# A linear-attention block and a gated feed-forward block in one kernel: how the start is fed, where M's last chunk is multiplied, and how the last token tile is split

## The chip, the cores and the metric

The kernel runs on one core of one Trainium2 chip. The core has a matrix engine (TensorE, PE in the profile; its weight loads are PEld), a vector engine (DVE), an activation engine (ScalarE, ACT), a general engine (GpSimd, POOL) and a queue engine (SyncE, SP), all with instruction streams of their own that wait for each other by semaphores. 16 DMA engines move data between HBM and the on-chip SBUF; matmuls write to PSUM, which has 8 banks. The metric is the device time of one execution in microseconds, lower is better.

## What is computed

`x` is 2048 tokens of 576 features in bf16. The output is `x` plus two branches that both start from the layer norm of `x`: a linear attention with 32 heads of 18 features, and a feed-forward block with 4608 hidden features.

```python
xn = layernorm(x)                                  # mean and variance over 576 features
q, k, v = split(xn @ wqkv)                         # 32 heads of 18
phi = lambda t: where(t > 0, t + 1, exp(t)) + 1e-6
kv  = einsum("bhsd,bhse->bhde", phi(k), v)         # 18 x 18 for each head
z   = sum over tokens of phi(k)
o   = einsum(phi(q), kv) / (einsum(phi(q), z) + 1e-6)
out = x + o @ wo + (gelu(xn @ w_gate) * (xn @ w_up)) @ w_down
```

## The kernel before

The kernel works in three stages on tiles of 128 tokens.

**Attention stage.** For each of 16 token tiles: load `x`, mean and variance (`bn_stats`, `bn_aggr`, VectorE), `rstd`, normalize into `xn`, transpose into `xnT` (on TensorE for the first two tiles, by DMA for the others), multiply by the k and q weights (four groups of five matmuls of 288 columns), apply phi (an exp on ScalarE, a min/max on VectorE), and accumulate `G = xn^T phi(k)`. kv follows from G at the end. `z` is added up on GpSimd. The instructions are put in order by a small list scheduler in the kernel that works with estimated durations; only the order of its steps reaches the engines. The loads and the layer norm:

```python
    load_x(0, 1)
    load_x(1, 1)
    nc.scalar.preload_act_table_set("natural_log_exp_and_others")
    load_w(1)
    load_x(2, 2)
    load_w(0)
    load_x(4, 4)
# ... (cut)
    def ln_rstd(n):
        r = rstd[:, n:n + 1]
        nc.gpsimd.tensor_scalar_add(out=r, in0=mv[:, n, 1:2], scalar1=EPS_LN)
        nc.gpsimd.tensor_tensor(out=r, in0=r, in1=mhalf[:], op=ALU.pow)

    def ln_bias(n):
        nc.gpsimd.tensor_scalar(
            out=nbias[:, n:n + 1], in0=mv[:, n, 0:1], scalar1=rstd[:, n:n + 1], scalar2=-1.0, op0=ALU.mult, op1=ALU.mult,
        )

    def ln_norm_act(n, c0=0, c1=D):
        nc.scalar.activation(
            out=xn[:, n, c0:c1], in_=x_sb[:, n, c0:c1], func=ACT.Identity, bias=nbias[:, n:n + 1], scale=rstd[:, n:n + 1],
        )

    def ln_norm(n, c0=0, c1=D):
        nc.vector.tensor_scalar(
            out=xn[:, n, c0:c1], in0=x_sb[:, n, c0:c1], scalar1=mv[:, n, 0:1], scalar2=rstd[:, n:n + 1],
            op0=ALU.subtract, op1=ALU.mult,
        )
```

The steps given to the scheduler, where `NORM` says for each token tile whether VectorE (D) or ScalarE (A) normalizes it:

```python
    def step(name, *args, **kw):
        steps[name] = _Step(*args, **kw)

    NORM = "DADADAAADAADAADA"
    COPY = ("DVE", "ACT")
# ... (cut)
    for n0 in range(8, NS, 2):
        step(("x", n0), "SP", 0.50, n0 - 5.5, [], lambda n0=n0: load_x(n0, 2), ready=1.6 * n0 + 2.0, tail=3.0)
    for n in range(NS):
        lead = {0: -9.0, 1: 0.5, 2: -0.5, 3: -0.5}.get(n, 0.0)
        after_x = [("x", n // 2 * 2)] if n >= 8 else []
        x_at = X_AT[n] if n < 8 else 0.0
        for h in range(2):
            step(("stats", n, h), "DVE", 0.41, n - 2.2 + lead, after_x, lambda n=n, h=h: ln_half(n, h), ready=x_at)
        step(("aggr", n), "DVE", 0.21, n - 2.1 + lead, [("stats", n, 0), ("stats", n, 1)], lambda n=n: ln_aggr(n))
        step(("rstd", n), "POOL", POW, n - 2.1 + lead, [("aggr", n)], lambda n=n: ln_rstd(n))
        if n < TD:
            for i, (k0, k1, eng) in enumerate([(0, 3, "ACT"), (3, KT, COPY[n])]):
                b = TP_BANK[n] - i
                if NORM[n] == "A":
                    if not i:
                        step(("bias", n), "POOL", 0.15, n - 2.1 + lead, [("rstd", n)], lambda n=n: ln_bias(n))
                    step(("norm", n, i), "ACT", (0.49, 0.36)[i], n - 2.1 + lead, [("bias", n)],
                         lambda n=n, k0=k0, k1=k1: ln_norm_act(n, k0 * P, min(k1 * P, D)))
                else:
                    step(("norm", n, i), "DVE", (0.27, 0.20)[i], n - 2.1 + lead, [("rstd", n)],
                         lambda n=n, k0=k0, k1=k1: ln_norm(n, k0 * P, min(k1 * P, D)))
# ... (cut)
                     lambda n=n, k0=k0, k1=k1, b=b, eng=eng: tp_copy(n, k0, k1, b, acopy if eng == "ACT" else vcopy))
            ready = [("xnT", n, 0), ("xnT", n, 1)]
        else:
            if NORM[n] == "A":
                step(("bias", n), "POOL", 0.15, n - 2.1, [("rstd", n)], lambda n=n: ln_bias(n))
                step(("norm", n), "ACT", 0.65, n - 2.1, [("bias", n)], lambda n=n: ln_norm_act(n))
            else:
                step(("norm", n), "DVE", 0.43, n - 2.1, [("rstd", n)], lambda n=n: ln_norm(n))
# ... (cut)
        if n > 0:
            idle = [("norm" if NORM[n + 4] == "D" else "bias", n + 4)] if n + 4 < NS else []
            step(("z", n), "POOL", 1.40, n + 2.0, [("phi", m, 1, h) for m in (0, n) for h in range(2)] + idle,
                 lambda n=n: z_add(n))
        step(("G", n), "PE", 0.75, n + 1.15, [("phi", n, 1, 0), ("phi", n, 1, 1)], lambda n=n: g_accumulate(n, G_A))
    step(("spin",), "PE", 0.11, -1.0, [("tp", 0, 1)], lambda: spin(2))

    step(("bmask",), "POOL", 0.95, 0.2, [("rstd", 2)], make_bmask)
    step(("g",), "POOL", 0.75, 0.3, [("rstd", 2)], clear_g)
```

**Gate/up stage.** It runs four times, for 512 tokens each: 18 blocks of two units, a unit being 18 matmuls of 64 rows by 512 columns. The array is split into two row tiles (partitions 0 to 63 and 64 to 127) that work at the same time on two PSUM banks. In `p1` one row tile adds to one bank and the other to the second; in `p2` they take the other bank each, after a no-op on another engine's queue has seen the last of `p1`:

```python
        def p1(self):
            for kt in self.first:
                self.mm(0, LO, kt, kt == self.first[0], False)
                last = self.mm(1, HI, kt, kt == self.first[0], False)
            self.turn = self.relay.nop()
            tc.add_manual_dep(self.turn.ins, last.ins.name, SYNC, reason="the row tiles take turns on a bank")

        def p2(self):
            for kt in self.then:
                m = self.mm(1, LO, kt, False, kt == self.then[-1])
                if kt == self.then[0]:
                    tc.add_manual_dep(m.ins, self.turn.ins.name, SYNC, reason="the bank's other row tile has written")
                self.mm(0, HI, kt, False, kt == self.then[-1])
# ... (cut)
            load_wo()
        elif sc == 0 and k >= 2:
            load_wd_slice()
        for i, (b, u) in enumerate(units):
            u.p2()
            gl = fwork.tile([P, SC], F32, name="gl")
            nc.scalar.activation(out=gl[:], in_=ps_all[:, b[0], :], func=ACT.Gelu_apprx_tanh)
            nc.vector.tensor_tensor(out=hT[:, GUB * k + i, :], in0=ps_all[:, b[1], :], in1=gl[:], op=ALU.mult)
```

During the first of the four, `M = kv @ wo` is made for the last four heads (72 rows) and copied to `m_last`, from which DMAs fill places in `m_sb`:

```python
    def load_wo():
        nc.sync.dma_start(wo2[:CR, 0:4, :], A_wo[0:4 * CR, :].rearrange("(c p) j -> p c j", p=CR))
        nc.sync.dma_start(wo2[:D - 4 * CR, 4, :], A_wo[4 * CR:D, :])
# ... (cut)
    def m_product(c, bank):
        rows = DH * HCH[c]
        for hf in range(2):
            b = bank(hf)
            hs = slice(hf * HALF, (hf + 1) * HALF)
            nc.tensor.matmul(
                ps_all[:rows, b, :HALF], lhsT=kvT[:rows, c, :rows], rhs=wo2[:rows, c, hs], start=True, stop=True,
            )
            nc.scalar.copy(out=m_sb[:rows, c, hs] if c < 4 else m_last[:rows, hs], in_=ps_all[:rows, b, :HALF])

    def m_last_product():
        two = [banks.next(), banks.next()]
        m_product(4, lambda hf: two[hf])

    def m_last_tails():
        for i in range(2):
            nc.sync.dma_start(m_sb[CR + i:CR + i + 1, 0:4, :], m_last[HP + 4 * i:HP + 4 * i + 4, :])

    def m_last_rows():
        for rows in (LO, HI):
            nc.sync.dma_start(m_sb[rows, 4, :], m_last[0:HP, :])

    m_last_steps = {4: m_last_product, 7: m_last_tails, 9: m_last_rows}
```

**Down stage.** For each of four token tiles, 36 matmuls with `w_down` and 4 with `M` for each half of 288 output columns, a pair of row-tiled matmuls for M's last chunk, the addition of `x`, and the store. The very last tile stores its halves apart:

```python

        def __init__(self, n):
            self.n, self.ts = n, slice(n * P, (n + 1) * P)
            self.banks = [banks.next(), banks.next()]
            self.opened = False
# ... (cut)
        def pair(self):
            for hf, rows in ((0, LO), (1, HI)):
                nc.tensor.matmul(
                    self.acc(hf), lhsT=pqT[rows, 4, self.ts], rhs=m_sb[rows, 4, HALVES[hf]],
                    start=not self.opened, stop=self.opened, skip_group_check=True,
                )
            self.opened = True
# ... (cut)
            for f in range(NF):
                if f in todo:
                    todo[f]()
                nc.tensor.matmul(
                    self.acc(hf), lhsT=hT[:, f, j * P:(j + 1) * P], rhs=wd_sb[:, f, HALVES[hf]],
                    start=(f == 0 and not paired), stop=False, skip_group_check=True,
                )
            for c in range(4):
                nc.tensor.matmul(
                    self.acc(hf), lhsT=pqT[:, c, self.ts], rhs=m_sb[:, c, HALVES[hf]],
                    start=False, stop=(paired and c == 3), skip_group_check=True,
                )

        def add(self, hf):
            if hf == 0:
                self.res = fwork.tile([P, D], BF16, name="res")
            hs = HALVES[hf]
            nc.vector.tensor_tensor(out=self.res[:, hs], in0=self.acc(hf), in1=x_sb[:, self.n, hs], op=ALU.add)
            if self.n == NS - 1:
                nc.sync.dma_start(out_view[:, self.n, hs], self.res[:, hs])
            elif hf == 1:
                nc.sync.dma_start(out_view[:, self.n, :], self.res[:])
```

Of the kernel before, what the change touches and what calls it, by code (L numbers as in the profile page):

```python
# [8 lines left out]
ACT = mybir.ActivationFunctionType  # L9
# [48 lines left out]
def kernel(  # L58
# [52 lines left out]
    load_x(1, 1)  # L111
# [9 lines left out]
    make_identity(nc, ident[:])  # L121
    eps_att = const.tile([P, 1], F32, name="eps_att")
    nc.vector.memset(eps_att[:], EPS_ATT)
    mhalf = const.tile([P, 1], F32, name="mhalf")
    nc.vector.memset(mhalf[:], -0.5)
# [12 lines left out]
    kvT = persist.tile([P, NCH, CR], BF16, name="kvT")  # L138
    pq = persist.tile([P, NS, D], BF16, name="pq")
# [37 lines left out]
    bmask = const.tile([P, CR], F32, name="bmask")  # L177
    g_sb = apool.tile([P, KT, D], BF16, name="g_sb")
    ones = const.tile([P, P], BF16, name="ones")

    def make_bmask():
        bm3 = bmask[:].rearrange("p (h e) -> p h e", e=DH)
        nc.gpsimd.memset(bmask[:], 1.0)
        nc.gpsimd.affine_select(
            out=bm3, in_=bm3, compare_op=ALU.is_ge, fill=0.0,
            base=0, pattern=[[-DH, 7], [0, DH]], channel_multiplier=1,
        )
        nc.gpsimd.affine_select(
            out=bm3, in_=bm3, compare_op=ALU.is_ge, fill=0.0,
            base=DH - 1, pattern=[[DH, 7], [0, DH]], channel_multiplier=-1,  # L190
        )

    def clear_g():
        nc.gpsimd.memset(g_sb[:, 4, :], 0.0)
        nc.gpsimd.memset(ones[:], 1.0)

# [23 lines left out]
    def ln_rstd(n):  # L220
        r = rstd[:, n:n + 1]
        nc.gpsimd.tensor_scalar_add(out=r, in0=mv[:, n, 1:2], scalar1=EPS_LN)
        nc.gpsimd.tensor_tensor(out=r, in0=r, in1=mhalf[:], op=ALU.pow)  # L223
# [6 lines left out]
    def ln_norm_act(n, c0=0, c1=D):  # L230
        nc.scalar.activation(
            out=xn[:, n, c0:c1], in_=x_sb[:, n, c0:c1], func=ACT.Identity, bias=nbias[:, n:n + 1], scale=rstd[:, n:n + 1],
        )
# [204 lines left out]
    NORM = "DADADAAADAADAADA"  # L438
    COPY = ("DVE", "ACT")
    POW = 0.55  # L440
    X_AT = [3.05, 3.50, 6.40, 6.40] + [9.50] * 4
    W_AT = {1: 5.60, 0: 8.00}
# [3 lines left out]
    for n in range(NS):  # L446
# [6 lines left out]
        step(("rstd", n), "POOL", POW, n - 2.1 + lead, [("aggr", n)], lambda n=n: ln_rstd(n))  # L453
        if n < TD:
            for i, (k0, k1, eng) in enumerate([(0, 3, "ACT"), (3, KT, COPY[n])]):
                b = TP_BANK[n] - i
                if NORM[n] == "A":
                    if not i:
                        step(("bias", n), "POOL", 0.15, n - 2.1 + lead, [("rstd", n)], lambda n=n: ln_bias(n))
                    step(("norm", n, i), "ACT", (0.49, 0.36)[i], n - 2.1 + lead, [("bias", n)],  # L460
                         lambda n=n, k0=k0, k1=k1: ln_norm_act(n, k0 * P, min(k1 * P, D)))
                else:
                    step(("norm", n, i), "DVE", (0.27, 0.20)[i], n - 2.1 + lead, [("rstd", n)],
                         lambda n=n, k0=k0, k1=k1: ln_norm(n, k0 * P, min(k1 * P, D)))
# [5 lines left out]
        else:  # L470
            if NORM[n] == "A":
# [16 lines left out]
        if n > 0:  # L488
            idle = [("norm" if NORM[n + 4] == "D" else "bias", n + 4)] if n + 4 < NS else []
            step(("z", n), "POOL", 1.40, n + 2.0, [("phi", m, 1, h) for m in (0, n) for h in range(2)] + idle,  # L490
                 lambda n=n: z_add(n))
        step(("G", n), "PE", 0.75, n + 1.15, [("phi", n, 1, 0), ("phi", n, 1, 1)], lambda n=n: g_accumulate(n, G_A))
    step(("spin",), "PE", 0.11, -1.0, [("tp", 0, 1)], lambda: spin(2))

    step(("bmask",), "POOL", 0.95, 0.2, [("rstd", 2)], make_bmask)
    step(("g",), "POOL", 0.75, 0.3, [("rstd", 2)], clear_g)
# [85 lines left out]

    def load_wo():
# [178 lines left out]
```

## Time and profile before

| | |
|---|---|
| time, median of three runs | 515.4 us (514.67 to 515.61) |
| span of the profiled execution | 513.7 us |
| attention stage, to the last k/q matmul | about 60.8 us |
| G's last tiles, kv | to 69.4 us |
| gate/up, each of four times | 69.9 us in the last three, 70.8 us in the first |
| down, each of four times | 39 to 40 us |
| granted TensorE clock | full speed in all slices |

The page of the profile gives each engine's busy time, the span in 40 slices, the chain of work that ended last (followed back from the last instruction, at each step to what released it), and the costliest groups of instructions. Here is its slice table; each digit is the busy share of one fortieth of the span (12.8 us) in tenths:

```
PE   7999999999999999999999999999999999999997
DVE  6896446554500045555300155555100356544100
ACT  4767533223320023233100022322000133232000
POOL 6567300000000000000000000000000000000000
DMA  6453919999800057756400166667100456540000
```

The first five slices are the attention stage, the only one in which all engines work. L12 in a profile line means line 12 of the kernel; matmuls are pipelined and their ends are modelled, so the distance of their starts says more than their lengths.

### The profile page before, as it was taken

The numbers are of one execution on the slowest core, as the hardware profiler recorded it, in microseconds if no ns is written. First come the engines' busy times: TensorE is split into PE (matmuls) and PEld (weight loads), VectorE is DVE, ScalarE is ACT, GpSimd is POOL, SyncE is SP. The second block draws the span as 40 slices with busy tenths as digits, with TensorE's granted clock in tenths as the row PEclk, the third lists the DMA queues.
The fourth block names the chain that finished last, engine by engine and source line by source line (L and its number), as shares of the span: only waits on it lengthen the run. The fifth ranks groups of instructions, "written<-read, shape, count | busy, mean of one in ns | idle before, by whom it ended". The sixth has DMA issues, their size and how long they took to land.

```text
span 513.7 us, 10671 instructions
## 1 busy us (share of the span) xinstructions
PE 506.6 (99%) x4487; PEld 306.4 (60%) x4487; DVE 210.7 (41%) x443; ACT 133.5 (26%) x239; POOL 38.2 (7%) x73
## 2 busy tenths in 40 slices
PE   7999999999999999999999999999999999999997
PEld 6877864444487744444677644444777444445775
DVE  6896446554500045555300155555100356544100
ACT  4767533223320023233100022322000133232000
POOL 6567300000000000000000000000000000000000
PEclk9999999999999999999999999999999999999999
DMA  6453919999800057756400166667100456540000
GB/s 208 99 112 55 254 48 270 283 232 279 212 13 13 1 151 165 161 154 172 106 11 13 50 175 168 168 160 151 47 16 1 141 153 174 162 130 15 13 11 24
DMA packets 119003, 61.27 MB, mean 119 GB/s; under 512 B 25570, under 2 KB 118122, under 8 KB 118954
## 3 DMA queue, kind: packets, MB, share of 16 engines
q1 hardware_dynamic: 118954, 60.58, 45.7%
q8 instruction: 35, 0.57, 0.5%
q14 instruction: 14, 0.11, 0.1%
HBM read 52.86 MB, written 2.36 MB: 108 GB/s over the span
## 4 chain that ended last, share of the span: by engine, by line
PE 93%; DVE 3%; DMA 1%; POOL 1%; issue 1%; ACT 1%; SPq 0%; ACTq 0%
PE ps_all L328 54%; PE ps_all L684 28%; PE ps_all L266 4%; PE ps_all L689 3%; PE ps_all L297 2%; DMA wqkv_sb<-in_A_wqkv_dram 1%; DVE pq L278 1%; DVE hT L278 1%; DVE stats L215 1%; ACT phi_e L273 1%; POOL z_sum L201 0%; PE ps_all L672 0%; PE ps_all L304 0%; DVE xn L236 0%; POOL rstd L223 0%
## 5 line engine op out<-in xcount | busy, mean ns | idle before, releaser
L328 PE MATMUL ps_all<-xnT,wg 64*128 64x512 bf16 x1152 | 272.0, 376 | 0.0
L328 PE MATMUL ps_all<-xnT,wu 64*128 64x512 bf16 x1152 | 271.5, 376 | 0.0
L624 ACT ACTIVATE gl<-ps_all 128x512 f32<-128x512 f32 x144 | 86.0, 597 | 311.2 <-PE ps_all L328 311.2
L625 DVE TENSOR_TENSOR hT<-ps_all,gl 128x512 bf16<-128x512 f32 x144 | 99.6, 692 | 131.1 <-ACT gl L624 130.8
L328 PEld LDWEIGHTS <-wu 64*128 64x128 bf16 x1152 | 108.4, 94 | 68.2
L328 PEld LDWEIGHTS <-wg 64*128 64x128 bf16 x1152 | 108.4, 94 | 67.7
L684 PE MATMUL ps_all<-wd_sb,hT 128*128 128x288 bf16 x1152 | 147.1, 286 | 0.0
L684 PEld LDWEIGHTS <-hT 128*128 128x128 bf16 x1152 | 112.3, 98 | 29.3 <-issue 1.2
L698 DVE TENSOR_TENSOR res<-ps_all,x_sb 128x288 bf16<-128x288 f32 x32 | 13.8, 455 | 146.4 <-PE ps_all L689 88.2
L328 PE MATMUL ps_all<-xnT,wr 64*128 64x512 bf16 x288 | 54.7, 376 | 0.0
L266 PE MATMUL ps_all<-wqkv_sb,xnT 128*128 128x288 bf16 x320 | 42.2, 286 | 2.3 <-DMA wqkv_sb<-in_A_wqkv_dram 1.4
L266 PEld LDWEIGHTS <-xnT 128*128 128x128 bf16 x320 | 30.6, 98 | 10.3 <-issue 2.7
L273 ACT ACTIVATE phi_e<-ps_all,neg 128x288 f32<-128x288 f32 x64 | 30.2, 496 | 10.7 <-PE ps_all L266 7.6
L328 PEld LDWEIGHTS <-wr 64*128 64x128 bf16 x288 | 14.0, 94 | 16.8 <-issue 0.2
L689 PE MATMUL ps_all<-m_sb,pqT 128*128 128x288 bf16 x128 | 20.9, 286 | 0.0
L297 PE MATMUL ps_all<-hT,xn 128*128 128x288 bf16 (+4 forms) x144 | 18.8, 274 | 0.0
L278 DVE SCALAR_TENSOR_TENSOR pq<-phi_e,ps_all 128x288 bf16<-128x288 f32 x32 | 13.8, 446 | 9.0 <-ACT phi_e L273 9.0
L201 POOL TENSOR_TENSOR z_sum<-z_sum,hT 128x576 f32<-128x576 f32 x13 | 16.3, 1250 | 6.7 <-DVE hT L278 6.6
L297 PEld LDWEIGHTS <-xn 128*128 128x128 bf16 x144 | 14.0, 98 | 3.6 <-issue 0.2
L278 DVE SCALAR_TENSOR_TENSOR hT<-phi_e,ps_all 128x288 bf16<-128x288 f32 x32 | 14.2, 453 | 3.6 <-ACT phi_e L273 3.4
L689 PEld LDWEIGHTS <-pqT 128*128 128x128 bf16 x128 | 12.5, 98 | 3.2
L215 DVE BATCH_NORM_STATS2 stats<-x_sb 128x6 f32<-128x288 bf16 x32 | 13.6, 438 | 1.6 <-DMA x_sb<-in_A_x_dram 1.6
(62 smaller groups left out, 133.1 us busy)
## 6 DMA issues: line engine op xcount, KB each, us to landing
wg<-in_B_w_gate_dram SPq DMA_DIRECT2D x72, 256.0 KB, 3.0
wu<-in_B_w_up_dram SPq DMA_DIRECT2D x72, 256.0 KB, 3.5
wd_sb<-in_B_w_down_dram SPq DMA_DIRECT2D x12, 432.0 KB, 5.1
wr<-in_B_w_gate_dram SPq DMA_DIRECT2D x72, 32.0 KB, 2.9
wr<-in_B_w_up_dram SPq DMA_DIRECT2D x72, 32.0 KB, 3.1
out_dram<-res SPq DMA_DIRECT2D x15, 144.0 KB, 1.8
wqkv_sb<-in_A_wqkv_dram SPq DMA_DIRECT2D x3, 576.0 KB, 4.7
x_sb<-in_A_x_dram SPq DMA_DIRECT2D x5, 288.0 KB, 3.7
```

The source lines that it names most:

```text
L201: nc.gpsimd.tensor_tensor(out=z_bf[:] if n == NS - 1 else z_sum[:], in0=pk[:, 0, 1:D + 1] if n == 1 else z_sum[:], in1=pk[:, n, 1:D + 1], ...
L215: nc.vector.bn_stats(out=ln_raw[n][:, h, :], in_=x_sb[:, n, h * HALF:(h + 1) * HALF])
L266: nc.tensor.matmul(ps_all[:, KQ_BANK[which] + hf, :HALF], lhsT=xnT[:, kt, n * P:(n + 1) * P], rhs=wqkv_sb[:, kt, c:c + HALF], start=(kt == ...
L273: nc.scalar.activation(out=e[:], in_=ps_all[:, KQ_BANK[which] + hf, :HALF], func=ACT.Exp, bias=neg1[:], scale=1.0,)
L278: nc.vector.scalar_tensor_tensor(out=(pq, pk)[which][:, n, which + hf * HALF:which + (hf + 1) * HALF], in0=e_tiles[n, which, hf][:], scala ...
L297: nc.tensor.matmul(ps_all[:, b, col:col + w], lhsT=xn[:, n, kt * P:(kt + 1) * P], rhs=pk[:, n, 1 + d0:1 + d0 + w], start=(n == 0 and col = ...
L328: return nc.tensor.matmul(self.outs[i], lhsT=self.lhs(i, rows, kt), rhs=self.rhs(i, rows, kt), start=start, stop=stop, skip_group_check=True,)
L624: nc.scalar.activation(out=gl[:], in_=ps_all[:, b[0], :], func=ACT.Gelu_apprx_tanh)
L625: nc.vector.tensor_tensor(out=hT[:, GUB * k + i, :], in0=ps_all[:, b[1], :], in1=gl[:], op=ALU.mult)
L684: nc.tensor.matmul(self.acc(hf), lhsT=hT[:, f, j * P:(j + 1) * P], rhs=wd_sb[:, f, HALVES[hf]], start=(f == 0 and not paired), stop=False, ...
L689: nc.tensor.matmul(self.acc(hf), lhsT=pqT[:, c, self.ts], rhs=m_sb[:, c, HALVES[hf]], start=False, stop=(paired and c == 3), skip_group_ch ...
L698: nc.vector.tensor_tensor(out=self.res[:, hs], in0=self.acc(hf), in1=x_sb[:, self.n, hs], op=ALU.add)
```

## The change

The change has several parts. (a) The load of token tile 1 is issued from ScalarE's queue instead of the sync queue. (b) `rstd` is made by Ln and Exp on ScalarE instead of an addition and a power on GpSimd. (c) Who normalizes which token tile is plain alternation: ScalarE the odd tiles from 3 on, VectorE the others. (d) The head mask `bmask` and the zeros of `g_sb` are set at the start, and the estimates given to the scheduler are others. (e) M's last chunk is made as a row-tiled unit inside gate/up's block 4: its 72 rows are split in 64 + 8, with zeros behind the 8, so that the array's split isn't changed for it. (f) The last token tile's output columns are parted 448 and 128 instead of 288 and 288, so that what is left after the last matmul is smaller.

The diff, cut to its core:

```diff
 
     load_x(0, 1)
-    load_x(1, 1)
+    load_x(1, 1, nc.scalar)
     nc.scalar.preload_act_table_set("natural_log_exp_and_others")
... (cut)
+    nc.gpsimd.memset(kvT[HP:P, 4, :], 0.0)
... (cut)
 
     def ln_rstd(n):
         r = rstd[:, n:n + 1]
-        nc.gpsimd.tensor_scalar_add(out=r, in0=mv[:, n, 1:2], scalar1=EPS_LN)
-        nc.gpsimd.tensor_tensor(out=r, in0=r, in1=mhalf[:], op=ALU.pow)
+        nc.scalar.activation(out=r, in_=mv[:, n, 1:2], func=ACT.Ln, bias=eps_ln[:], scale=1.0)
+        nc.scalar.activation(out=r, in_=r, func=ACT.Exp, scale=-0.5)
... (cut)
-    NORM = "DADADAAADAADAADA"
-    COPY = ("DVE", "ACT")
-    POW = 0.55
-    X_AT = [3.05, 3.50, 6.40, 6.40] + [9.50] * 4
-    W_AT = {1: 5.60, 0: 8.00}
+    X_AT = [3.65, 4.20, 6.40, 6.40] + [9.50] * 4
+    W_AT = {1: 5.50, 0: 7.60}
... (cut)
-        step(("rstd", n), "POOL", POW, n - 2.1 + lead, [("aggr", n)], lambda n=n: ln_rstd(n))
+        step(("rstd", n), "ACT", 0.49, n - 2.1 + lead, [("aggr", n)], lambda n=n: ln_rstd(n))
         if n < TD:
-            for i, (k0, k1, eng) in enumerate([(0, 3, "ACT"), (3, KT, COPY[n])]):
+            for i, (k0, k1, eng) in enumerate([(0, 3, "ACT"), (3, KT, "ACT" if n else "DVE")]):
                 b = TP_BANK[n] - i
-                if NORM[n] == "A":
-                    if not i:
-                        step(("bias", n), "POOL", 0.15, n - 2.1 + lead, [("rstd", n)], lambda n=n: ln_bias(n))
-                    step(("norm", n, i), "ACT", (0.49, 0.36)[i], n - 2.1 + lead, [("bias", n)],
-                         lambda n=n, k0=k0, k1=k1: ln_norm_act(n, k0 * P, min(k1 * P, D)))
-                else:
-                    step(("norm", n, i), "DVE", (0.27, 0.20)[i], n - 2.1 + lead, [("rstd", n)],
-                         lambda n=n, k0=k0, k1=k1: ln_norm(n, k0 * P, min(k1 * P, D)))
+                step(("norm", n, i), "DVE", 0.25, n - 2.1 + lead, [("rstd", n)],
+                     lambda n=n, k0=k0, k1=k1: ln_norm(n, k0 * P, min(k1 * P, D)))
... (cut)
-            if NORM[n] == "A":
+            if n % 2:
                 step(("bias", n), "POOL", 0.15, n - 2.1, [("rstd", n)], lambda n=n: ln_bias(n))
                 step(("norm", n), "ACT", 0.65, n - 2.1, [("bias", n)], lambda n=n: ln_norm_act(n))
... (cut)
         if n > 0:
-            idle = [("norm" if NORM[n + 4] == "D" else "bias", n + 4)] if n + 4 < NS else []
+            idle = [("norm", n + 4) if n % 2 == 0 else ("bias", n + 4)] if n + 4 < NS else []
             step(("z", n), "POOL", 1.40, n + 2.0, [("phi", m, 1, h) for m in (0, n) for h in range(2)] + idle,
                  lambda n=n: z_add(n))
         step(("G", n), "PE", 0.75, n + 1.15, [("phi", n, 1, 0), ("phi", n, 1, 1)], lambda n=n: g_accumulate(n, G_A))
... (cut)
 
+    nc.gpsimd.memset(wo2[HP:P, 4, :], 0.0)
+
     def load_wo():
... (cut)
         units = []
+        aside = m_last_unit() if blk == 4 else None
+        if aside:
+            aside.p1()
         for i in range(GUB):
             b = [banks.next(), banks.next()]
... (cut)
             load_wd_slice()
+        if aside:
+            aside.p2()
+            m_last_copy(aside)
         for i, (b, u) in enumerate(units):
... (cut)
-
-    def m_last_product():
+            nc.scalar.copy(out=m_sb[:rows, c, hs], in_=ps_all[:rows, b, :HALF])
+
+    def m_last_unit():
+        rows4 = DH * HCH[4]
         two = [banks.next(), banks.next()]
-        m_product(4, lambda hf: two[hf])
+        outs = [ps_all[:rows4, b, :HALF] for b in two]
+        return _Unit(
+            outs, lambda i, rows, kt: kvT[rows, 4, :rows4], lambda i, rows, kt: wo2[rows, 4, i * HALF:(i + 1) * HALF],
+            nc.gpsimd, first=(0,), then=(0,),
+        )
+
+    def m_last_copy(u):
+        for i in range(2):
+            nc.scalar.copy(out=m_last[:DH * HCH[4], i * HALF:(i + 1) * HALF], in_=u.outs[i])
 
     def m_last_tails():
         for i in range(2):
... (cut)
-    m_last_steps = {4: m_last_product, 7: m_last_tails, 9: m_last_rows}
-
-    HALVES = [slice(0, HALF), slice(HALF, D)]
+    m_last_steps = {7: m_last_tails, 9: m_last_rows}
+
+    LAST_MID = 448
... (cut)
             self.n, self.ts = n, slice(n * P, (n + 1) * P)
             self.banks = [banks.next(), banks.next()]
             self.opened = False
+            mid = LAST_MID if n == NS - 1 else HALF
+            self.parts = [slice(0, mid), slice(mid, D)]
 
         def acc(self, hf):
-            return ps_all[:, self.banks[hf], :HALF]
+            return ps_all[:, self.banks[hf], 0:self.parts[hf].stop - self.parts[hf].start]
 
... (cut)
-                    self.acc(hf), lhsT=pqT[rows, 4, self.ts], rhs=m_sb[rows, 4, HALVES[hf]],
+                    self.acc(hf), lhsT=pqT[rows, 4, self.ts], rhs=m_sb[rows, 4, self.parts[hf]],
... (cut)
-            hs = HALVES[hf]
+            hs = self.parts[hf]
             nc.vector.tensor_tensor(out=self.res[:, hs], in0=self.acc(hf), in1=x_sb[:, self.n, hs], op=ALU.add)
             if self.n == NS - 1:
                 nc.sync.dma_start(out_view[:, self.n, hs], self.res[:, hs])
```

(Cut are the constants for epsilon, further lines around the mask and the zeros, and the places where `HALVES` becomes `self.parts` in the same way.)

## The prediction

> **What bounds the kernel now.** I read the page first: the shares of the engines, then the chain that ended last.
>
> ```profile
> PE 506.6 (99%) x4487; PEld 306.4 (60%) x4487; DVE 210.7 (41%) x443; ACT 133.5 (26%) x239; POOL 38.2 (7%) x73
> ...
> PE 93%; DVE 3%; DMA 1%; POOL 1%; issue 1%; ACT 1%; SPq 0%; ACTq 0%
> ```
>
> TensorE carries the span. The row-tiled gate/up matmuls (L328, 54% of the chain) and the full down matmuls (L684 and L689, 31%) run from 69 us to the end, nearly without gaps, and the change touches only two spots there. So a large gain is out of reach; what can move is the first 60 us, one seam in gate/up, and the tail. Next I looked at what TensorE waited for, over the whole run:
>
> ```profile
> PE ps_all L132 <- POOL ident masks.py:199: 1.4, 1, 1.4
> PE ps_all L266 <- DMA wqkv_sb<-in_A_wqkv_dram: 1.4, 1, 1.4
> PE ps_all L266 <- DVE pq L278: 0.6, 2, 0.4
> PE ps_all L266 <- ACT xnT L255: 0.2, 1, 0.2
> ```
>
> The columns are total us, times, longest. In the attention stage the one sizeable wait is 1.4 us for the q weights; after it, 0.6 us for phi. By the windows of busy time, the stretch from the landing of these weights to the last k/q matmul looks so:
>
> ```profile
> 10.09:60.81 50.72, 50.00 (x417) 40.14 (x417) 38.02 (x103) 35.59 (x70) 31.18 (x53) 1.00 0.54 121
> ```
>
> The columns are us, then PE, PEld, DVE, ACT and POOL busy. The busy PE includes modelled overlap, so I count its work from starts: 310 L266 matmuls and 15 tiles of L297. Twenty L266 take 2.45 us (0.1227 each), seven L297 take 0.75 us. 310 x 0.1227 + 15 x 0.75 = 49.3 us of 50.7. At most 1.4 us can be won inside this stretch; VectorE and ScalarE have 25 to 30% spare on average.
>
> The seam in gate/up, in order of time (start, length):
>
> ```profile
> 88.57 0.38 PE L328 MATMUL ps_all<-xnT,wu 64*128 64x512 bf16 x1
> 88.58 0.38 PE L328 MATMUL ps_all<-xnT,wg 64*128 64x512 bf16 x1
> ...
> 88.88 0.44 PE L635 MATMUL ps_all<-wo,kvT 72*72 72x288 bf16 x2
> ...
> 89.25 0.39 PE L328 MATMUL ps_all<-xnT,wr 64*128 64x512 bf16 x2
> ```
>
> Row-tiled pairs start every 0.213 us. The next one would have started at 88.79, but it started at 89.25: M's last chunk costs 0.46 us, of which the two 288-column matmuls explain 0.245.
>
> **What the Trainium skill says.** Four places bear on this. (1) TensorEngine Tiling (Array Packing), Key Properties: changing the tiling mode, as against the tile, drains TensorE. The trace agrees: 0.46 - 0.245 = 0.21 us are lost on two mode changes here. (2) ScalarE: Activation LUTs, What ACT_TABLE_LOAD costs: an ACTIVATE has a fixed part, 280 ns when its bias is a per-partition operand, plus 0.833 ns per element, and neighbours overlap by some 93 ns. Our phi exp of 288 columns took 496 ns; 280 + 240 = 520 is close. (3) SBUF — State Buffer, Who interferes with whom: VectorE in a two-port mode and GpSimd exclude each other for whole instructions. The trace agrees: the normalization of 576 elements (L236) took 0.42 us alone and 1.39 us at 34.46, while GpSimd's z addition ran from 34.39. (4) DMA: Bandwidth & Descriptors, Issuing engines are not separate DMA queues: a second issuing engine saves issue time alone. The trace has all issues on one queue, so it can't show it, but from 4 to 9 us the DMA share is 0.91 to 1.11, so there is no spare bandwidth to be found.
>
> **The change part by part.**
>
> 1. *x tile 1 issued from ScalarE's queue.* The sync queue's issues took 0.43 to 0.57 us each, in a row from 0.79 us. Taking one out moves all later issues forward by some 0.45 us: Wk, x 2-3, Wq. Wq's landing at 10.05 is partly issue, partly bandwidth; I give it 0.3 us. Against this, x 0 and x 1 now share the engines from the start and x 0 lands later. The schedule's constants in the diff say so too: 3.65 for x 0 against 3.05, 4.20 against 3.50 for x 1, 7.60 against 8.00 for Wq. A later x 0 is harmless: tile 0's k matmuls started at 6.61 and ended at 8.0, two us ahead of Wq. So **-0.3 us**.
>
> 2. *rstd by Ln and Exp on ScalarE instead of add and power on GpSimd.* Removed from GpSimd: 16 x (0.22 + 0.57) = 12.7 us, none of it bounding. Added on ScalarE: two one-column activations per tile. From (2) each has little but the fixed part; two that depend on each other, with an overlap before and after, come to an estimate of 0.5 us per tile; the 14 tiles from n = 2 on give 7 us. Latency of one rstd falls from some 1.0 us (4.09 to 5.10 at tile 0) to 0.6, but now it stands in a queue with the exps.
>
> 3. *Norms: odd tiles from 3 on ScalarE, the others on VectorE.* For n >= 2 ScalarE goes from 9 to 7 norms (-2 x 0.78 at their pace = -1.6 us), VectorE from 5 to 7 (+2 x 0.42). ScalarE in the 50.7 us stretch: 35.6 + 7 - 1.6 = 41.0, 81%; VectorE: 38.0 + 0.85 = 38.9, 77%. But LN work ends at 48 us: from 10 to 50 us ScalarE has 29.1 of 40 us busy now (the sum of four windows of 10 us: 6.99, 7.68, 6.78, 7.64), and 34.5, or 86%, then. An in-order engine at 86%, with exps behind rstds and norms, gives late phis now and then, and a late phi is what TensorE waited for in the two 'DVE pq' waits. More norms on VectorE also mean more chances for the 1.39 us clash with GpSimd. I expect TensorE's stalls in the stretch to grow from 1.4 to some 2.4 us: **+1.0 us**. This is the least certain term; the balance before (a string of D and A for each tile) looks chosen for evenness, and the change goes back to plain alternation.
>
> 4. *bmask, g_sb and ones set up at the start.* About 1.75 us of GpSimd moved from behind tile 2's rstd to the front. No rstd stands behind it on GpSimd any more. **0**.
>
> 5. *M's last chunk as a row-tiled unit.* Four 288-column matmuls in two concurrent pairs, 2 x 0.123 us, the same as two full ones; both mode changes go: **-0.2 us**. Its operands are needed at the start of block 4 (about 85 us) instead of its end (88.9); the load of wo is issued at 75.7 to 76.7, early enough. Its two copies to m_last, some 0.39 us each, run beside the next 0.85 us of matmuls, ahead of the first gelu.
>
> 6. *Last token tile in parts of 448 and 128 columns.* 40 matmuls of 448 at (448/2.4 + 2.6 ns, the pace that 288 columns show) and 40 of 128 at 56 ns give 7.57 + 2.24 = 9.81 us, what 2 x 4.9 us were before; twenty 126-column matmuls of the kv stage took 1.11 us, 55 ns each, so weight loads don't hold them up. The pair's row tiles run as long as the longer, 448 against 288: +0.06. The last add has 128 columns instead of 288: two rows of the page, 455 ns at 288 and 692 at 512, give 1.06 ns per column, so -0.17. The last store has 32 KB instead of 72; stores of 144 and 72 KB landed in 1.8 and 1.6 us, so -0.1 at best. Together **-0.2 us**.
>
> Sum: -0.3 + 1.0 - 0.2 - 0.2 = +0.3 us on 515.4: **515.7 us**.
>
> **The rivals.** *The start wins and nothing is given back.* GpSimd is relieved and z finishes sooner; VectorE and ScalarE keep 14 to 23% spare, and the single wait of 1.4 us for Wq shrinks. For it: in the second half of the stretch, from 43 us, TensorE ran without any gap. Then only the gains stand, -0.7 us, and the present stalls may shrink a little too: about 514.5 us. *ScalarE becomes the bound of the attention stage.* At 86% and with chained Ln and Exp, each of some tiles' q and k banks are freed late; 12 tiles with 0.2 to 0.3 us each would be +3 us, about 517.5 us. Against it: the two banks of k and of q come round only every 3.2 us, while exp and phi take 0.95, so a tile has 1.6 us of slack (3.2 - 0.61 - 0.95). *The start is bound by bandwidth and not by issue.* Then part 1 gives 0, and if x 0 comes so late that tile 0 isn't done before Wq, it costs; 516 us.
>
> **Range and chances.** Fixed by arithmetic are parts 5 and 6 (-0.4, give or take 0.15). Open are the landing of Wq (0 to -0.5) and the stalls (-0.7 to +3). Three times before lie within 0.9 us of each other. I take 514.2 to 517.4 us. Two per cent are 10.3 us, over three times the largest rival's term, so within 2%: 0.98; faster 0.01, slower 0.01.
>
> **What would show it.** Right: the seam in block 4 closes (row-tiled pairs 0.213 us apart with only 0.25 us inserted and no gap); the last add takes about 0.29 us; the wait for Wq ends at about 9.7; ScalarE's busy time over the stretch is about 41 us; TensorE's waits for phi sum to 1 to 2 us. Wrong: TensorE waiting for xnT of tile 0 or 1 in place of Wq (part 1); a stretch from the first q matmul to the last k/q matmul that is still 50.7 us or shorter (part 3); 128-column matmuls slower than 56 ns (part 6); a wait ahead of the row-tiled unit for wo or for its turn (part 5).

## The result and the profile after

The changed kernel takes 512.45 us (median of 4 runs, 512.27 to 512.72) where the kernel before, measured beside it, takes 515.5: a ratio of 0.9944, 95% interval 0.9926 to 0.9961, or 2.9 us less. Predicted were 515.7 us, with a range of 514.2 to 517.4. Small as it is, the gain lies outside the range, and it came from the stretch for which a loss was forecast.

The two traces fall into these parts, read from the starts in the chain of the kernel:

| part (us) | before | after | difference |
|---|---|---|---|
| to the start of q's matmuls | 10.09 | 8.80 | -1.29 |
| from there to the last k/q matmul | 50.72 | 49.53 | -1.19 |
| the rest of the attention stage | 8.61 | 8.60 | -0.01 |
| the first gate/up stage | 70.75 | 70.53 | -0.22 |
| from its end to the end of the span | 373.53 | 373.24 | -0.29 |

Shares of the engines and the chain of the kernel after:

```profile
PE 505.2 (99%) x4489; PEld 304.6 (60%) x4489; DVE 211.4 (41%) x447; ACT 136.9 (27%) x267; POOL 25.5 (5%) x40
...
PE 98%; DMA 1%; SPq 0%; issue 0%; DVE 0%
```

VectorE, ScalarE and GpSimd held 5% of the chain before and have gone from it. TensorE's waits over the whole run, after:

```profile
PE ps_all L132 <- POOL ident masks.py:199: 1.4, 1, 1.4
PE ps_all L248 <- DVE xn L233: 0.6, 1, 0.6
PE ps_all L263 <- DMA wqkv_sb<-in_A_wqkv_dram: 0.3, 1, 0.3
PE ps_all L263 <- ACT xnT L252: 0.3, 1, 0.3
```

The wait for the q weights is 0.3 us instead of 1.4, and no wait for phi is left. The stretch from q to the last k/q matmul, in the view of windows (us, then PE, PEld, DVE, ACT, POOL busy):

```profile
8.80:58.33 49.53, 49.53 (x419) 40.22 (x419) 39.51 (x109) 39.51 (x97) 19.72 (x22) 1.00 0.51 115
```

ScalarE does 3.9 us more than before and TensorE does not wait for it. From here on, 'stalls' is the time from the first q matmul to the start of whatever follows the last k/q matmul, less the 49.3 us of work that the prediction counted: 60.65 - 10.09 - 49.3 = 1.3 us before, 58.16 - 8.80 - 49.3 = 0.1 after (the two late transposes of tile 1). The chain above takes a modelled end in place of a start, which adds 0.2 us to both.

The seam and the tail, in order of time:

```profile
84.48 0.38 PE L325 MATMUL ps_all<-xnT,wg 64*128 64x512 bf16 x1
...
84.69 0.29 PE L325 MATMUL ps_all<-wo,kvT 64*72 64x288 bf16 x2
...
84.82 0.38 PE L325 MATMUL ps_all<-xnT,wu 64*128 64x512 bf16 x1
...
497.81 6.97 PE L688 MATMUL ps_all<-wd_sb,hT 128*128 128x448 bf16 x36
...
505.38 2.17 PE L688 MATMUL ps_all<-wd_sb,hT 128*128 128x128 bf16 x36
...
507.81 0.29 DVE L702 TENSOR_TENSOR res<-ps_all,x_sb 128x128 bf16<-128x128 f32 x1 [1.61 <-PE ps_all L693]
```

The second half of M's row-tiled unit takes 0.13 us between its neighbours, 84.69 to 84.82, without a gap (its first half stands at 82.41 to 82.54). The 36 matmuls of 128 columns start 55.8 ns apart (505.38 to the next group's start at 507.39), and the last add takes 0.29 us instead of 0.46.

### The profile page after: what moved, and what is told of

The parts are those of the page before. It is cut to its first block, busy times and chain, and to the rows that moved or that the text cites. A ratio compares the mean times of both kernels' runs of the same rounds, so it can differ in the third digit from the quotient of the medians.

```text
span 510.7 us, 10656 instructions
## 1 busy us (share of the span) xinstructions
PE 505.2 (99%) x4489; PEld 304.6 (60%) x4489; DVE 211.4 (41%) x447; ACT 136.9 (27%) x267; POOL 25.5 (5%) x40
## 4 chain that ended last, share of the span: by engine, by line
PE 98%; DMA 1%; SPq 0%; issue 0%; DVE 0%
PE ps_all L325 55%; PE ps_all L688 28%; PE ps_all L263 7%; PE ps_all L294 3%; PE ps_all L693 3%; DMA wqkv_sb<-in_A_wqkv_dram 1%; PE ps_all L676 0%; PE ps_all L301 0%; PE ps_all L374 0%; PE ps_all L628 0%; SPq L93 0%; SPq L108 0%; SPq L107 0%; DVE res L702 0%; PE ps_all L362 0%
## 5 line engine op out<-in xcount | busy, mean ns | idle before, releaser
L688 PE MATMUL ps_all<-wd_sb,hT 128*128 128x288 bf16 (+2 forms) x1152 | 147.1, 286 | 0.0
L688 PEld LDWEIGHTS <-hT 128*128 128x128 bf16 x1152 | 110.8, 98 | 30.9 <-issue 1.2
L702 DVE TENSOR_TENSOR res<-ps_all,x_sb 128x288 bf16<-128x288 f32 (+2 forms) x32 | 13.8, 455 | 146.3 <-PE ps_all L693 88.1
L693 PE MATMUL ps_all<-m_sb,pqT 128*128 128x288 bf16 (+2 forms) x128 | 20.9, 286 | 0.0
```

Source lines behind the costliest of these rows:

```text
L688: nc.tensor.matmul(self.acc(hf), lhsT=hT[:, f, j * P:(j + 1) * P], rhs=wd_sb[:, f, self.parts[hf]], start=(f == 0 and not paired), stop=Fa ...
L693: nc.tensor.matmul(self.acc(hf), lhsT=pqT[:, c, self.ts], rhs=m_sb[:, c, self.parts[hf]], start=False, stop=(paired and c == 3), skip_grou ...
```

## The experiments

Three groups: what each part is worth, why the layer norm's part helped, why the start did. All ratios are to the kernel before on the same chip, with 95% intervals; 0.001 is 0.5 us. 'q at 9.40' means that the first q matmul started at 9.40 us in the profiled run.

### What each part is worth

**The load alone** (e1), on the kernel before:

```diff
-    load_x(1, 1)
+    load_x(1, 1, nc.scalar)
```

> The kernel before with one edit: x tile 1 is loaded from ScalarE's queue. Theory (the queue feeds the q weights sooner): Wq lands at about 8.8 us instead of 10.05, and the time falls by 1.0 to 1.4 us, to about 514.2. Rival 1 (only the issue time is saved): Wq lands 0.45 us sooner, -0.4 us. Rival 2 (the late landing before was one slow DMA engine by chance, or belongs to the layer norm's order): no change, 515.4.

Measured: 1.0006 (0.9998 to 1.0014), so no gain, which is the second rival's number. The profile shows why. q starts at 9.40 instead of 10.09, but the last k/q matmul ends later than before (61.17 us against 60.65): the stalls are 2.5 us. In order of time:

```profile
13.02 0.27 POOL L226 TENSOR_SCALAR nbias<-mv,rstd 128x1 f32<-128x1 f32 x1
13.32 0.87 ACT L231 ACTIVATE xn<-x_sb,nbias,rstd 128x576 bf16<-128x576 bf16 x1 [1.38 <-POOL nbias L226]
13.97 0.29 PE L297 MATMUL ps_all<-hT,xn 128*128 128x288 bf16 x1
14.09 1.26 ACT L273 ACTIVATE phi_e<-ps_all,neg 128x288 f32<-128x288 f32 x3
14.61 0.46 DVE L278 SCALAR_TENSOR_TENSOR hT<-phi_e,ps_all 128x288 bf16<-128x288 f32 x1 [0.89 <-ACT phi_e L273]
...
15.12 0.79 PE L297 MATMUL ps_all<-hT,xn 128*128 128x289 bf16 x6 [0.86 <-DVE hT L278]
```

Read it upwards from the last line: TensorE waits for a phi, VectorE for its exp, and the exp stands in ScalarE's queue behind a norm that waited 1.38 us for GpSimd's bias. The weights came sooner, the layer norm did not.

**All but the load** (e2): the changed kernel with `load_x(1, 1)` back on the sync queue.

> The changed kernel with x tile 1 back on the sync queue, all else as changed. Theory: the q weights land near 10 us again and the time rises by 1.0 to 1.4 us, to about 513.6. Rival 1 (issue time only): +0.4, 512.9. Rival 2 (chance, or the order of the layer norm): 512.5, as changed.

Measured: 513.62 us, 0.9964 (0.9952 to 0.9977), against 0.9944 for the whole change: the load is worth about 1.0 us here. q starts at 9.73, stalls 0.1.

**The layer norm's part alone** (e3), on the kernel before:

```diff
-        nc.gpsimd.tensor_scalar_add(out=r, in0=mv[:, n, 1:2], scalar1=EPS_LN)
-        nc.gpsimd.tensor_tensor(out=r, in0=r, in1=mhalf[:], op=ALU.pow)
+        nc.scalar.activation(out=r, in_=mv[:, n, 1:2], func=ACT.Ln, bias=eps_ln[:], scale=1.0)
+        nc.scalar.activation(out=r, in_=r, func=ACT.Exp, scale=-0.5)
 ... and the norms in alternation, the masks at the start; loads, M, last tile, arrival times as before
```

> The kernel before with the layer norm's part alone: rstd by Ln and Exp on ScalarE, plain alternation of the norms, masks set at the start; x tile 1 stays on the sync queue, the M chunk and the last tile as before, and the scheduler's arrival times as before. Theory (the stalls after Wq came from ScalarE waiting in order for GpSimd's chain): TensorE's stalls after Wq fall from 1.4 us to under 0.3, the time by about 1.2 us, to 514.3. Rival (the order fitted to the other arrival times does it, not the engine that makes rstd): stalls stay at 1 us or more, 515.0 to 515.5. The prediction on record: +1.0 us, 516.4.

Measured: 514.07 us, 0.9973 (0.9962 to 0.9984), -1.4 us; q at 10.01, stalls 0.2. These are the theory's numbers.

**M's unit and the last tile alone** (e4): those parts of the diff on the kernel before, nothing else.

> The kernel before with M's last chunk as a row-tiled unit and the last tile in 448 and 128 columns, nothing else. The prediction on record says -0.4; the two traces show 0.22 at the first gate/up stage and 0.29 from there to the end. Theory: -0.5 us, 514.9. Rival (these stretches gained from the earlier start or from transfers lying elsewhere): 0 to -0.2 us.

Measured: 0.9993 (0.9985 to 1.0001), -0.4 us with an interval that touches zero; the traces of the two kernels give the sharper -0.5. The three parts, each taken where it was measured (the load on top of the others), sum to -1.4 - 1.0 - 0.4 = -2.8 of -2.9 us.

### Why the layer norm's part helped

**rstd on ScalarE alone** (e5): the first diff of e3 and the step's engine in the scheduler, nothing more.

> The kernel before with rstd made by Ln and Exp on ScalarE; which engine normalizes which tile, the masks, the loads and the rest stay as before. Theory (ScalarE stood in its own queue behind norms that waited for GpSimd's rstd chain): TensorE's stalls after the q weights (1.4 us before) fall below 0.5 us though ScalarE has more to do, time 514.3 to 514.6. Rival (it is the fewer norms on ScalarE and the plain alternation that help): stalls stay, or grow with ScalarE's load as the prediction had it, 515.5 to 516.5.

Measured: 514.23 us, 0.9980 (0.9972 to 0.9988); stalls 0.1, with ScalarE busy 34.8 of the 40 us from 10 to 50 us, more than in the changed kernel (33.6). So the new engine for rstd is enough, and ScalarE's load is not what stalls TensorE.

**The alternation alone** (e6), rstd still on GpSimd:

```diff
-    NORM = "DADADAAADAADAADA"
+    NORM = "DDDADADADADADADA"
```

> The kernel before with the norms in plain alternation as in the change (VectorE tiles 0, 1 and the even ones, ScalarE the odd ones from 3 on), rstd still on GpSimd. Theory: ScalarE still waits for GpSimd's chain at its 7 norms and VectorE at its 7; the stalls stay near 1.4 us, time within 0.5 us of before, 515.0 to 516.0. Rival (the alternation is what helps): stalls under 0.5 us, 514.4.

Measured: 516.58 us, 1.0026 (1.0015 to 1.0038), beyond both. But three of its six runs took 517.0 to 517.6 us at a mean granted clock of 0.996, the profiled one among them; the three at 0.999 to 1.0 took 515.9 to 516.2 us, about 0.5 us more than the kernel before, at the upper edge of the theory's range. In the profile stalls are 3.8 us, though ScalarE waited for the bias only 2.1 us in total, against 5.3 before. My theory that ScalarE's waits do it could not be the whole. Two waits of TensorE make 2.2 of the 3.8 us: 0.65 us ahead of the group at 27.07, where ScalarE's norm at 25.28 had waited 1.35 us for the bias, and 1.5 us ahead of the group at 29.19, right behind a long norm of VectorE. The other 1.7 us are the clock: after these waits TensorE was granted half of it from 29.7 to 33.1 us. VectorE's norms; start and length:

```profile
20.90 1.30 DVE L236 TENSOR_SCALAR xn<-x_sb,mv,rstd 128x576 bf16<-128x576 bf16 x1 [0.32 <-POOL rstd L223]
...
27.47 1.30 DVE L236 TENSOR_SCALAR xn<-x_sb,mv,rstd 128x576 bf16<-128x576 bf16 x1 [0.45 <-POOL rstd L223]
...
36.08 0.96 DVE L236 TENSOR_SCALAR xn<-x_sb,mv,rstd 128x576 bf16<-128x576 bf16 x1
```

Three of the seven norms of tiles 2 to 14 take two to three times their 0.43 us; the one at 27.47 is the one that TensorE waited behind.

**Almost no z** (e7): `z_add` returns at once for tiles 2 to 14; these are left out of z.

> The kernel before without 13 of the 15 z additions on GpSimd (tiles 2 to 14 are left out of z; only the first and last addition are made), so GpSimd has nothing between the rstds. If GpSimd's occupation by z (waits in its queue, and the port that it takes from VectorE) makes the stalls: they fall under 0.4 us, 514.4. If the length of the rstd and bias chain itself (0.22 + 0.57 + 0.26 us and the hand-overs) makes them, whatever z does: they stay at 1 us or more, 515.2.

Measured: 513.95 us, 0.9975 (0.9966 to 0.9985), without that part of the work; stalls 0.1, with rstd on GpSimd. All of VectorE's norms take at most 0.43 us and ScalarE's waits for the bias fall to 2.1 us. The rstd chain by itself is quick enough; what hurts is z on the same engine.

**Late norms moved to ScalarE** (e9): `NORM = "DADADAAAAAAAAAAA"` on the kernel before.

> The kernel before with the norms of tiles 8, 11 and 14 moved from VectorE to ScalarE, rstd still on GpSimd. This takes away the overlap of VectorE's norm with GpSimd's z addition (the 1.39 us norm at 34.46). If the shared port made the stalls: they fall from 1.3 us to under 0.7, 514.7. If it is the queue (ScalarE behind norms that wait for rstd, which waits behind z): they stay at 1.3 us or grow, as ScalarE has three more such waits, 515.3 to 516.3.

Measured: 514.27 us, 0.9984 (0.9977 to 0.9990); stalls 0.7. ScalarE's waits for the bias stayed (5.4 us, nine times) and half of the stalls went.

**z waits for the norm** (e13), on the kernel before:

```diff
+        if n + 4 in norm_ins:
+            tc.add_manual_dep(z.ins, norm_ins[n + 4].ins.name, SYNC, reason="z leaves the port to the norm")
```

> The kernel before with one added wait: GpSimd's z addition of tile n starts only when VectorE has normalized tile n + 4, where VectorE does that; engines, order and work stay as before. If the overlap of z with VectorE's norm makes the later stalls: the 1.39 us norm falls to 0.43, the two waits for phi of q (0.6 us) go, stalls fall from 1.3 to about 0.6 us, 514.5 to 514.8. If not: stalls stay at 1.3 us, 515.2, or grow by z running late.

Measured: 514.13 us, 0.9976 (0.9966 to 0.9985). One added wait makes the kernel 1.2 us faster. The same moment in the kernel before, in order of time:

```profile
33.85 0.57 POOL L223 TENSOR_TENSOR rstd<-rstd,mhalf 128x1 f32<-128x1 f32 x1
...
34.39 1.29 POOL L201 TENSOR_TENSOR z_sum<-z_sum,hT 128x576 f32<-128x576 f32 x1
34.46 1.39 DVE L236 TENSOR_SCALAR xn<-x_sb,mv,rstd 128x576 bf16<-128x576 bf16 x1 [0.38 <-POOL rstd L223]
...
35.77 0.81 DVE L278 SCALAR_TENSOR_TENSOR pq<-phi_e,ps_all 128x288 bf16<-128x288 f32 x2
36.26 0.41 PE L266 MATMUL ps_all<-wqkv_sb,xnT 128*128 128x288 bf16 x2 [0.40 <-DVE pq L278]
```

and in e13:

```profile
33.79 0.57 POOL L225 TENSOR_TENSOR rstd<-rstd,mhalf 128x1 f32<-128x1 f32 x1
...
34.40 0.43 DVE L240 TENSOR_SCALAR xn<-x_sb,mv,rstd 128x576 bf16<-128x576 bf16 x1 [0.38 <-POOL rstd L225]
...
34.74 0.81 DVE L282 SCALAR_TENSOR_TENSOR pq<-phi_e,ps_all 128x288 bf16<-128x288 f32 x2
...
34.90 1.29 POOL L201 TENSOR_TENSOR z_sum<-z_sum,hT 128x576 f32<-128x576 f32 x1 [0.54 <-DVE xn L240]
```

GpSimd's next instruction after rstd is z. The end of rstd releases VectorE's norm and, in GpSimd's own queue, z; z is there first by 0.07 us, and the norm ends 0.17 us after z does. The two phis behind it come 1 us late and TensorE waits. With z held back all five norms of the stretch take 0.43 us or less and the stalls are 0.6 us.

That is only half of the 1.2 us: q also began 0.38 us sooner in this trace, which the added wait doesn't explain. e4 serves as a control here. Its attention stage is that of the kernel before, but for one memset at the start, and its q began at 9.67 us (e13: 9.71). Its stalls are 1.7 us and its last k/q work ends at 60.67 us, like the kernel before's (60.65); e13's ends at 59.63. An earlier q alone gains nothing there, and the added wait gains 1.0 us at the same q.

The 0.6 us that remain are two waits for a phi, ahead of the groups at 14.49 and 42.40 us. The second stands in the kernel before too, at 43.42, behind ScalarE's wait for the bias:

```profile
39.06 1.20 POOL L201 TENSOR_TENSOR z_sum<-z_sum,hT 128x576 f32<-128x576 f32 x1
39.10 0.20 DVE L218 BATCH_NORM_AGGREGATE mv<-stats 128x2 f32<-128x12 f32 x1
...
40.35 0.22 POOL L222 TENSOR_SCALAR rstd<-mv 128x1 f32<-128x1 f32 x1
...
41.62 0.87 ACT L231 ACTIVATE xn<-x_sb,nbias,rstd 128x576 bf16<-128x576 bf16 x1 [0.84 <-POOL nbias L226]
...
42.40 1.65 ACT L273 ACTIVATE phi_e<-ps_all,neg 128x288 f32<-128x288 f32 x4
42.91 0.85 DVE L278 SCALAR_TENSOR_TENSOR pq<-phi_e,ps_all 128x288 bf16<-128x288 f32 x2 [0.86 <-ACT phi_e L273]
...
43.42 0.77 PE L266 MATMUL ps_all<-wqkv_sb,xnT 128*128 128x288 bf16 x5 [0.23 <-DVE pq L278]
```

The tile's statistics are there at 39.30, but GpSimd is busy with z until 40.26 and begins rstd at 40.35. ScalarE's norm waits for the bias made from it, the exps stand behind the norm, VectorE's phi waits for an exp and TensorE for the phi: the order seen in e1. So both paths begin with z on the engine that makes rstd. ScalarE's waits for the bias are 5.7 us in e13, 2.1 in e7 and 0.8 in e5, the last two with stalls of 0.1; but e5 and e7 remove both paths at once or shorten both, so the share of this second path is read from the order of the lines, and no run isolates it.

### Why the start helped

**Tiles 0 and 1 in one load** (e8), on the changed kernel:

```diff
-    load_x(0, 1)
-    load_x(1, 1, nc.scalar)
+    load_x(0, 2)
```

> The changed kernel with x tiles 0 and 1 in one transfer on the sync queue: one issue less than with two, like the change, but no second queue. Theory A (the saved issue slot, 0.45 us early in the row, is what brings Wq forward): Wq lands at about 8.8 to 9.0 us as with the change, 512.5 to 512.8. Theory B (the second queue is what helps, its packets fill the engines in parallel): Wq lands near 9.7 as with tile 1 on the sync queue, 513.5.

Measured: 512.55 us, 0.9942 (0.9929 to 0.9956), as the change; q at 9.11. No second queue is needed.

**One tiny issue more** (e12), on the changed kernel:

```diff
     load_x(0, 1)
+    nc.sync.dma_start(spare_t[:], x_view[0:16, 0, 0:64])
     load_x(1, 1, nc.scalar)
```

> The changed kernel with one more small transfer (16 rows of 128 bytes, used by nothing) issued on the sync queue between x tile 0 and Wk; x tile 1 stays on ScalarE's queue. If the place in the row of issues decides when Wq lands: the dip of the DMA rate at 3.0 to 3.5 us comes back and Wq lands near 9.7, 513.2 to 513.6. If it is x tile 1's 147 KB in that queue ahead of Wk: Wq lands at about 8.8 plus at most 0.45 us of later issue, 512.5 to 512.9.

Measured: 513.4 us, 0.9961 (0.9947 to 0.9974); q at 9.87. 2 KB that nobody uses cost as much as putting tile 1 back (e2): the place in the row of issues counts, not the bytes. The rate of the DMA engines in three half-microseconds (the last number of a line, GB/s) shows what follows. Before:

```profile
2.50:3.00 0.50, 0.50 (x8) 0.50 (x7) 0.00 (x0) 0.00 (x0) 0.46 (x1) 1.00 1.09 313
3.00:3.50 0.50, 0.50 (x7) 0.50 (x6) 0.47 (x2) 0.00 (x0) 0.50 (x1) 1.00 1.00 131
3.50:4.00 0.50, 0.50 (x8) 0.50 (x6) 0.47 (x2) 0.00 (x0) 0.33 (x3) 1.00 0.80 219
```

After:

```profile
2.50:3.00 0.50, 0.50 (x8) 0.50 (x7) 0.00 (x0) 0.01 (x1) 0.39 (x3) 1.00 0.96 332
3.00:3.50 0.50, 0.50 (x7) 0.50 (x6) 0.00 (x0) 0.00 (x0) 0.50 (x1) 1.00 1.05 337
3.50:4.00 0.50, 0.50 (x8) 0.50 (x6) 0.14 (x1) 0.00 (x0) 0.47 (x1) 1.00 1.08 373
```

In all ten profiles with two issues ahead of Wk (before, e2 to e7, e9, e12, e13) the rate is 74 to 198 GB/s from 3.0 to 3.5 us; in the five with one (after, e1, e8, e11, e14) it is 325 to 353. From 3.0 to 4.0 us the kernel before moves 0.5 x (206 + 154) = 180 KB less than the changed one, half a microsecond at 350 GB/s. But it had moved more just before (237 GB/s against 71 from 2.0 to 2.5 us), so at 4.0 us it is some 107 KB behind, 0.3 us. By 9.0 us it is some 230 KB behind, 0.65 us; a third of that comes from 6 to 7 us, at 294 against 372 GB/s. The 0.44 us by which Wk is issued later can't be added to this, as the low rate may be its effect. So the bytes account for about half of the 1.29 us between the two traces. Why the engines, shown as busy, move so little there was not settled.

One pair of traces is also no good measure of the start: in the eight profiles whose loads are those of the kernel before, q began anywhere from 9.16 (e6) to 10.25 us (e7). The times of e2 and e12 carry this finding, at ratios of 0.9964 and 0.9961 against 0.9944 for the change.

**Tile 1 between Wk's two transfers** (e10), on the changed kernel: `load_w(1)` with `load_x(1, 1)` between its large and its small part.

> The changed kernel with x tile 1 on the sync queue, but issued between the large and the small transfer of Wk: as many issues ahead of Wq as with tile 1 in its old place, but only one ahead of Wk. If the number of issues ahead of Wq decides: Wq lands at about 9.7 us, 513.5. If the dip of the DMA rate at 3.0 to 3.5 us (111 to 131 GB/s with two issues ahead of Wk, 325 to 344 with one) decides, because the engines run dry before Wk is there: the dip is gone, Wq lands at 9.0 to 9.3, 512.6 to 512.9.

Measured: 514.52 us, 0.9984 (0.9977 to 0.9991), and inconclusive for its question: tile 1's statistics wait for its data until 6.12, VectorE does them ahead of tile 0's norm, and TensorE stands still for 2.0 us, to 7.28. Its granted clock is then 0.56 from 8 to 9 us and 0.50 from 9 to 11, and tile 0's ten k matmuls take 2.58 us instead of 1.40. The DMA rate from 3.0 to 3.5 us is 182 GB/s although only one issue stands ahead of Wk, so that the engines run dry before Wk is not the explanation of the low rate, or not the whole of it.

**x 2-3 behind Wq** (e11), on the changed kernel: `load_w(0)` ahead of `load_x(2, 2)`, arrival times to match.

> The changed kernel with x tiles 2 and 3 loaded behind Wq instead of ahead of it (295 KB, 0.8 us at 370 GB/s), and the scheduler's arrival times set to match. If Wq alone still binds the start: q of tile 0 starts at about 8.2 instead of 8.8 and the time falls by 0.4 to 0.6 us, to 512.0. If tile 2 then comes too late for its layer norm and transposing DMA: the gain is lost to a wait for xnT, 512.5 or more.

Measured: 512.79 us, 0.9952 (0.9940 to 0.9965). q at 8.64, not 8.2; stalls 0.5. The scheduler's order changed with its arrival times, and 0.3 us of waiting for phi took the place of the gain.

**Wq from ScalarE's queue** (e14), on the changed kernel: both transfers of Wq issued there behind tile 1.

> The changed kernel with both transfers of Wq issued from ScalarE's queue behind x tile 1, so that the sync queue has x 0, Wk, x 2-3 alone ahead. If the place in the row of issues still costs: q of tile 0 starts at 8.2 to 8.5 instead of 8.8 us, time 512.0 to 512.3, the best so far. If the two weights now share the engines' time and Wk lands later: k of tile 0 starts after 7.2 instead of 6.9 and the gain is lost, 512.4 to 513.0.

Measured: 514.10 us, 0.9982 (0.9975 to 0.9988), worse than both expectations:

```profile
8.80 0.82 DVE L212 BATCH_NORM_STATS2 stats<-x_sb 128x6 f32<-128x288 bf16 x2 [1.95 <-DMA x_sb<-in_A_x_dram]
9.65 0.21 DVE L215 BATCH_NORM_AGGREGATE mv<-stats 128x2 f32<-128x12 f32 x1
9.78 0.57 DVE L233 TENSOR_SCALAR xn<-x_sb,mv,rstd 128x384 bf16<-128x384 bf16 x2
```

The two weights share the engines, x 2-3 lands at 8.8 (with the change its statistics started at 6.76), and VectorE's queue has that tile's statistics ahead of tile 1's norm; q starts at 10.34. No version tried beats the changed kernel; e8 equals it.

## Why the prediction was wrong

**Step 3, the sign.** The prediction said +1.0 us of new stalls, from an in-order ScalarE at 86%. The load was forecast well (34.5 us of the 40, measured 33.6) and the conclusion was false: stalls went from 1.3 to 0.1 us. e5 runs at 34.8 us without stalls. What stalled the kernel before were hand-overs from GpSimd, and both stood in the profile of the kernel before: ScalarE's norms waited 5.3 us, seven times, for the bias, and the norm of 1.39 us was even quoted under the port rule. I charged the port clash to the change, as 'more chances' with more norms on VectorE. But a clash needs GpSimd to begin z just as the norm is released, and it does so because rstd, which releases the norm, is GpSimd's instruction ahead of z. By taking rstd off GpSimd the change took the cause away. The longest of the seven norms of tiles 2 to 14 is 0.57 us after, though there are two more of them. Clashes are not excluded by it: one norm of e5 took 0.88 us, with no stall behind it. Alternation without that move (e6) did meet more clashes, and its loss of 1.1 us is close to my +1.0; but that is no support for the step, since ScalarE was busy only 26.5 of the 40 us there, and the runs at full clock lost only some 0.5 us. The sign that the prediction named against this step, a stretch of 50.7 us or shorter, is what came: 49.5. Of the 3.2 us between the forecast change (+0.3) and the measured one (-2.9), this step makes 2.4 (+1.0 against -1.4 in e3) and step 1 makes 0.7.

**Step 2, called harmless.** "None of it bounding" was said of GpSimd's 12.7 us of rstd, from its share of busy time. GpSimd was no bound, but two engines waited for it by turns.

**Step 1, the size.** -0.3 us was forecast, q started 1.29 us sooner in the pair of traces, and the times of e2 and e12 put it at 1.0 and 0.9 us. The mis-sized term is the landing of Wq: I took at most 0.45 us of issue time and capped it by a bandwidth that I took as fixed, having read the DMA share (0.91 to 1.11) as full use. The rate between 3.0 and 3.5 us was 131 GB/s at a share of 1.00: a busy share isn't bytes. The Trainium skill (DMA: Bandwidth & Descriptors, Issuing engines are not separate DMA queues) fits e8, in that a second queue isn't what helps. But it says that only the issue time is saved, and e12 measures more: an issue of 0.44 us cost 0.9 us of time. The late x 0 was harmless, as said (tile 0's k at 6.91).

**Rivals.** The first, that nothing is given back, had the right direction; it failed by counting the gain of the stalls as 'a little'. The second, ScalarE as the bound, is refuted by e5 (busy 34.8 of 40 us, stalls of 0.1), the third, a start bound by bandwidth alone, by e2 and e12. The gains also aren't additive: the load alone (e1) gives nothing, since the stalls eat the start.

**Steps 4, 5 and 6.** The masks and zeros end on GpSimd at 5.83 us, ahead of its first bias at 11.40; no run moves them alone, but e3, which moves them, and e5, which doesn't, differ by 0.2 us, inside their intervals. Part 5 was -0.2, measured -0.22. Part 6 was -0.2, measured -0.29: add 0.46 to 0.29, the pair +0.06 (0.41 against 0.35 us from its start to the next matmul), 36 matmuls of 128 columns at 55.8 ns against 56; the 32 KB store landed in 1.4 us against 1.6.

## What to carry to other kernels

Before a change that moves small instructions between engines, list who waits for the engine that they leave, and what stands behind them in its queue: 0.8 us on an engine with time to spare can hold up two others. A long outlier in a group of equal instructions (1.39 us among 0.43) names a collision; find what starts both at once, and hold one back, as e13 does with one wait. The start of one trace can lie a microsecond off that of the next, so take a gain there from the times of several runs. At the start of a kernel, count the issues ahead of the first large transfer and look at the bytes moved, not at the busy share.

## What the runs showed of the hardware

A 576-column bf16 norm on VectorE took 0.42 us alone and 1.30 to 1.39 us when GpSimd's addition had begun up to 0.07 us earlier; it then ended 0.15 to 0.17 us after that addition. An unused transfer of 2 KB ahead of a large one, 0.44 us of issue, cost 0.9 us of time (e12 against the changed kernel). TensorE, idle for 2.0 us up to 7.28 us (e10), was granted half of its clock from 8.1 to 11.5 us; an idle of 1.7 us up to 10.16 us (e14) left its clock whole.
